# Work of GpSimd moved to VectorE, of VectorE to ScalarE, in three stages of a fused attention and expert kernel

## The chip, the cores and the metric

The kernel runs on one core of a Trainium2 chip, as one program. Its engines are TensorE (PE, matmuls and transposes), VectorE (DVE), ScalarE (ACT) and GpSimd (POOL); SyncE (SP) issues most of the DMAs. Each engine works through its own queue in order, and semaphores tie them together. The metric is the device time of one execution in microseconds (us).

## The reference

Three layers follow one another. Attention with 32 heads (4 batches x 8) over 1152 keys of 64 numbers, where pairs of queries are averaged first, leaves 576 x 4 = 2304 tokens of 512 numbers. A dense layer follows, and then a choice of one of eight experts for each token:

```
q_pool = q.reshape(B, H, S // 2, 2, D).mean(axis=3)
attn = softmax(q_pool @ k.T / 8);  x = attn @ v            # 2304 tokens x 512
h = x @ w_in;  g = h * sigmoid(1.702 * h);  x = g @ w_out   # 2048 hidden units
do = x @ w_skip > 0;  e = argmax(x @ w_gate)                # one of 8 experts
x[do] += p[e] * (relu(x[do] @ w1[e]) @ w2[e])               # 1024 hidden units
```

The result has to be right to float32. w_in and w_out come as 64-bit floats, all else as 32-bit floats.

## The kernel before, in words

All large products run in float32r, TensorE's rounded float format. To keep the precision, each operand is split into a high part (rounded, a ScalarE copy) and a low part (the rest, a subtraction), and a product is three matmuls: high x high, high x low, low x high.

**Attention** goes over 16 pairs of heads, 14 score units to a pair. Python code writes out the order: an agenda (`Agenda`) holds work for a later unit, and `quiet` puts work only on the units named in `AV_AT`. Beside it, the weights of the first of the 16 slices of the dense layer (`EARLY = 1`) are loaded and split in single steps (`weights`, L341).

**Splitting 64-bit weights** (`wsplit`, L422). A weight is two 32-bit words, 8 bytes from one to the next. Instructions on words build the high part: and with 0x7FFFFFFF (L450), shift (L451), max (L452), shift-or of the low word (L440) and its scaled copy on ScalarE (L441), shift-and (L454), or of the sign (L455), sign word (L444), and the low part's multiply (L445). The copy into the high part (L446, the put) follows one step later. The instructions stand in a list fq, and `fill(k)` takes the next k from it.

**The dense layer** (`ffn`, L484) goes over six chunks of tokens, 768, 384, 256, 256, 256 and 384, and in each over the 16 slices of 128 hidden units; a chunk of 768 has two pieces of 384 to a slice. One step is one piece of one slice: `layer1` has twelve matmuls into h, then Sigmoid (ScalarE, L568), g (VectorE, L569), its high half gh (ScalarE, L570) and its low half gl (L572). `layer2` follows two steps later with nine matmuls of 512 columns for a piece of 384. The weights stay in memory for all chunks and are split in the first one only, one half of a slice per step: that is the first pass, 32 steps of 21 matmuls. fill runs three of the list's instructions between g and gl, and four behind gl. Beside the end of a chunk the tokens of the next one are loaded (`xload`, SP queue), normalized (`xnorm`, L469) and split (`xhigh`, `xlow`).

**The experts** (`experts`, L841) take up to eight experts in turn, a slot each, and the tokens of a slot in tiles of 128. `tokens_tile` computes one: `up` (24 matmuls into two halves of h, hp), relu, transposes, the halves of hT (L928, L929), `down` (24 matmuls), and yo, which GpSimd's indirect DMA writes to the tokens' rows. In the first tile of a slot the weights of the next expert are split, 16 pieces (`splits`, L892): each is one ScalarE copy (L800) and one subtraction (L801). They stand in the queues between the parts of the tile: 3, 2, 2 and 2 pieces ahead of the second half's hT, 7 behind it. A weight buffer (stage) holds two pieces, and the load of the next expert but one fills it when both are split.

Of the kernel before, what the change touches and what calls it, by code (L numbers as in the profile page):

```python
# [71 lines left out]
class Kernel:  # L72
# [349 lines left out]
    def wsplit(self, fq, a, tmp, fb, k, ag=None):  # L422

        nc, V = self.nc, self.nc.vector
        hi_t, lo_t = self.W[fb, ("wih", "woh")[k]], self.W[fb, ("wil", "wol")[k]]
        if a.dtype == F32:
            def plain():
                nc.scalar.activation(hi_t, a, AF.Copy)  # L430
                V.tensor_tensor(lo_t, a, hi_t, op=ALU.subtract)
            fq.append(plain)
            return
        w = a.bitcast(U32).rearrange("p (n two) -> p n two", two=2)
        lo, hi = w[:, :, 0], w[:, :, 1]
        t1, t2, sg = tmp
        least = float(np.uint32(0x38000000).view(np.float32))

        def low():
            V.scalar_tensor_tensor(t1, lo, 9, t1, op0=ALU.logical_shift_right, op1=ALU.bitwise_or)  # L440
            nc.scalar.activation(t1.bitcast(F32), t1, AF.Copy, scale=2.0 ** -43)  # L441

        def last():
            V.tensor_scalar(sg, t2, 0xFF800000, None, op0=ALU.bitwise_and)  # L444
            (nc.gpsimd if fb else V).tensor_tensor(lo_t, t1.bitcast(F32), sg.bitcast(F32), op=ALU.mult)  # L445
            put = lambda: nc.scalar.activation(hi_t, t2.bitcast(F32), AF.Copy)  # L446
            put() if ag is None else ag.at(ag.now + 1, put)

        fq += [
            lambda: V.tensor_scalar(t2, hi, 0x7FFFFFFF, None, op0=ALU.bitwise_and),  # L450
            lambda: V.tensor_scalar(t1, hi, 23, None, op0=ALU.logical_shift_left),  # L451
            lambda: V.tensor_scalar(t2.bitcast(F32), t2.bitcast(F32), least, None, op0=ALU.max),  # L452
            low,
            lambda: V.tensor_scalar(t2, t2, 3, 0x3FFFF000, op0=ALU.logical_shift_left, op1=ALU.bitwise_and),  # L454
            lambda: V.scalar_tensor_tensor(t2, hi, 0xC0000000, t2, op0=ALU.bitwise_and, op1=ALU.bitwise_or),  # L455
            last,
        ]
# [11 lines left out]
        eng.tensor_tensor(x[:, :n], t[:, 0, :n], t[:, 1, :n], op=ALU.mult)  # L469

    def xtile(self, c, j, pc):
        i = (j * 2 + pc) if len(pieces(CH[c])) == 2 else (j * 2 + c % 2)
        n = pieces(CH[c])[pc][1]
        return [self.xhl[k][i][:, :n] for k in range(2)]

# [8 lines left out]
    def ffn(self, ctx):  # L484
# [59 lines left out]

        def xnorm(c, j, pc):
            xa[c, j, pc] = xr.tile([P, 384], F32, name="xa", tag="xa", bufs=4)
            self.xnorm(xa[c, j, pc], xraw.pop((c, j, pc)), c, j, pc, nc.gpsimd)

        def xsplit(c, j, pc):
            self.xhigh(xa[c, j, pc], c, j, pc)  # L550
# [4 lines left out]
        def layer1(c, fb, pc, fa, fb_):  # L555
            n = pieces(CH[c])[pc][1]
            h = hp.tile([P, 512], F32, name="h", tag="h")[:, :n]
            ah, al = self.W[fb, "wih"], self.W[fb, "wil"]
            k = 0
            for d in range(ND):  # L560
                xh, xl = self.xtile(c, d, pc)
                for a, x in ((ah, xh), (ah, xl), (al, xh)):
                    nc.tensor.matmul(h, a[:, d * P:d * P + P], x, start=(k == 0), stop=(k == 3 * ND - 1))  # L563
                    k += 1
            g = gp.tile([P, 384], F32, name="g", tag="g")[:, :n]
            gh = g3.tile([P, 384], F32R, name="gh", tag="gh")[:, :n]
            gl = g3.tile([P, 384], F32R, name="gl", tag="gl")[:, :n]
            nc.scalar.activation(g, h, AF.Sigmoid, scale=1.702)  # L568
            V.tensor_tensor(g, h, g, op=ALU.mult)  # L569
            nc.scalar.activation(gh, g, AF.Copy)  # L570
            fill(fa)
            (nc.gpsimd if c == 0 else V).tensor_tensor(gl, g, gh, op=ALU.subtract)  # L572
            fill(fb_)
            G[c, fb, pc] = (gh, gl)

# [147 lines left out]
        for g in range(len(steps) + LAG):  # L723
            ag.now = g
            if g < len(steps):
                c, fb, pc = steps[g]
                fa, fb_ = (2, 3) if CH[c] >= 384 else (1, 2)
                if g == 2:
                    self.recip(sm, B - 1, ag, 3)
                if c == 0:  # L730
                    if pc == 0:
                        fill(99)
                    wload(2 * (fb + EARLY) + 3 + pc)
                    wsplit(2 * (fb + EARLY) + 1 + pc)
                    fa, fb_ = 3, 4
                layer1(c, fb, pc, fa, fb_)
                if fb == 0 and pc == 0 and c + 1 < len(CH):
                    for j in range(ND):
                        for q in range(len(pieces(CH[c + 1]))):
                            g0 = first[0, 10] + 2 * j if c == 0 else first[c, 4] + 2 * j  # L740
                            ag.at(g0, xload, c + 1, j, q)
                            ag.at(g0 + 1, xnorm, c + 1, j, q)
                            ag.at(first[c, NF - 1] + 1 if c == 0 else g0 + 4, xsplit, c + 1, j, q)
            if g >= LAG:
                c2, f2, p2 = steps[g - LAG]
                layer2(c2, f2, p2)
                if f2 == NF - 1:
                    if c2 == 0 and p2 == 0:
                        rctx.close()
                        late["o"] = self.pool(ctx, "m_o", 2)  # L750
                        late["wg"] = late["o"].tile([P, 9, DM], F32, name="wg", tag="wg", bufs=1)
                        dma(late["wg"][:, 0:8], self.wgT.partition_broadcast(P))
                        dma(late["wg"][:, 8], self.w_skip.partition_broadcast(P))
                        for d in range(ND):
                            dma(wgd[:, d, 0:8], self.wgT[:, d * P:d * P + P].rearrange("e p -> p e"))
                            dma(wgd[:, d, 8:9], self.w_skip[d * P:d * P + P].rearrange("(p a) -> p a", a=1))
                    o, n = pieces(CH[c2])[p2]
                    grp = tuple((C0[c2] + o) // P + i for i in range(n // P))
                    if c2 < len(CH) - 1:
                        todo.extend((grp, i) for i in range(len(grp)))  # L760
            if g < len(steps) + LAG - 1:
                rstep()
                ag.run(g)
            if not (self.first or todo or fq or live[0]) and self.listed == NT - CH[-1] // P:

                self.first = late["o"].tile([P, 9, DM], F32, name="first", tag="wg", bufs=1)
                for m in range(4):
                    self.first_expert_load(m)
                for m in range(8):
                    ag.at(max(g + 2 + m // 2, first[len(CH) - 1, m] + LAG + 1), self.first_expert_split, m)  # L770

                ps = hp.tile([P, 8], F32, name="cn", tag="h")
                nc.tensor.matmul(ps, ONE, mac[self.listed], start=True, stop=True)
                V.tensor_scalar(self.early, ps[:, 0:1], P - 0.5, float(P), op0=ALU.is_gt, op1=ALU.mult)
                dma(self.ids_e, self.LIST[0:P])
                V.memset(self.x_e, 0.0)
                nc.gpsimd.indirect_dma_start(
                    out=self.x_e, out_offset=None, in_=self.X2[0:C0[-1]],
                    in_offset=bass.IndirectOffsetOnAxis(ap=self.ids_e[:, 0:1].bitcast(U32), axis=0),
                    bounds_check=C0[-1] - 1, oob_is_err=False,  # L780
                )
# [13 lines left out]
        fb, k = (s % 2) * 8 + q // 2, q % 2  # L795
        return self.W[fb, ("wih", "woh")[k]], self.W[fb, ("wil", "wol")[k]]

    def expert_split(self, s, q, raw, eng):
        hi, lo = self.piece(s, q)
        self.nc.scalar.activation(hi, raw, AF.Copy)  # L800
        eng.tensor_tensor(lo, raw, hi, op=ALU.subtract)  # L801

    def first_expert_load(self, m):
        t = self.first[:, m % 4 * 2:m % 4 * 2 + 2]
# [4 lines left out]

    def first_expert_split(self, m):  # L810
        for c in range(2):
            self.expert_split(0, 2 * m + c, self.first[:, m % 4 * 2 + c], self.nc.vector)
        if m < 4:
            self.first_expert_load(m + 4)

# [25 lines left out]
    def experts(self, ctx):  # L841
# [48 lines left out]
                dma(t, src)  # L890

        def splits(s):  # L892
            return [
                lambda q=q: self.expert_split(s, q, stage[q // 2][:, q % 2], nc.gpsimd if q % 3 == 2 else V)
                for q in range(16)
            ]

        def xpose(t):
            p = take("pt", pt)
# [8 lines left out]
        def tokens_tile(s, t, id2, x, ahead=(), more=(), behind=()):  # L908
# [35 lines left out]
            turned(0)  # L944
            some(A2)
            up(1, (2, 3))
            V.tensor_scalar(h[:, 512:], hp[1], 0.0, None, op0=ALU.max)
            for tn, xx in ahead:
                xput(xpose(tn), xx)
            some(A3)  # L950
# [100 lines left out]
```

## Time and profile before

| | us |
|---|---|
| three runs | 1127.57, 1119.11, 1115.97; median 1119.11 |
| the profiled execution | 1114.21, span 1112.4 |
| busy: TensorE | 1017.9 (91%) |
| busy: VectorE | 806.9 (73%) |
| busy: GpSimd | 581.1 (52%) |
| busy: ScalarE | 482.1 (43%) |

Attention goes to some 449 us, the first pass from there to 629, the other chunks to 902, the experts to the end. The shares of busy time are means over stages with different limits; what holds a stage is read in that stage. TensorE's granted clock was 0.966 of 2.4 GHz in the mean.

### The profile page before, as it was taken

Reading aid. Unit: us, or ns where it says so; the run is one execution under the profiler, and the core shown is the slowest. Engines: PE = TensorE matmul, PEld = TensorE weight load, DVE = VectorE, ACT = ScalarE, POOL = GpSimd, SP = SyncE. Lnnn points to the kernel's source line nnn. Section 1 sums busy time; section 2 is a strip of 40 time slices with the busy share of each in tenths; the row PEclk is TensorE's granted clock in tenths of the full one; section 3 lists DMA queues with packets and bytes.
Section 4 is the critical chain, followed back from the end, with each engine's and each line's share of the span. In section 5 each row is a group of like instructions: output and inputs, shape, how many; then the busy total and the mean of one; then the engine's idle time right before and its main releaser. Section 6 shows DMA issues by size and latency. Waiting matters only on the chain. (4 is left out here: it accounts for less than half of the span.)

```text
span 1112.4 us, 19158 instructions
## 1 busy us (share of the span) xinstructions
PE 1017.9 (91%) x7002; PEld 801.3 (72%) x7002; DVE 806.9 (73%) x1584; ACT 482.1 (43%) x885; POOL 581.1 (52%) x408
## 2 busy tenths in 40 slices
PE   6999999999999999688978999999999989977893
PEld 4766767666776666587867898888889877755672
DVE  6767787778877772699999589787567555578734
ACT  2555555555555545243333332333332334256432
POOL 3698888998999988444445202101110106156413
PEclk9999999999999999889999999999999989988897
DMA  4233332223333210332333420211211326456301
GB/s 154 66 95 80 92 108 77 76 90 91 92 108 93 71 48 27 125 96 95 105 117 100 143 77 20 69 62 31 66 41 55 111 92 215 149 184 214 112 31 39
DMA packets 64325, 103.39 MB, mean 93 GB/s; under 512 B 18630, under 2 KB 34630, under 8 KB 64072
## 3 DMA queue, kind: packets, MB, share of 16 engines
q1 hardware_dynamic: 60148, 96.35, 27.4%
q0 software_dynamic: 3904, 5.15, 1.5%
q8 instruction: 69, 1.13, 0.4%
q14 instruction: 56, 0.46, 0.1%
q10 hardware_dynamic: 148, 0.30, 0.1%
HBM read 90.04 MB, written 17.35 MB: 97 GB/s over the span
## 5 line engine op out<-in xcount | busy, mean ns | idle before, releaser
L230 DVE TENSOR_REDUCE mx<-xs 128x1 f32<-128x384 f32 x432 | 213.0, 549 | 79.5 <-PE xs L227 74.8
L271 ACT ACTIVATE E<-ss 128x640 f32<-128x640 f32 (+1 forms) x224 | 174.0, 786 | 155.3 <-PE ss L270 123.0
L286 POOL TENSOR_TENSOR acc<-acc,E 128x640 f32<-128x640 f32 (+1 forms) x96 | 182.1, 1897 | 19.5 <-ACT E L271 15.4
L563 PE MATMUL h<-xh,wih 128*128 128x384 f32 (+1 forms) x448 | 145.8, 326 | 30.8 <-ACT wih L446 26.0
L306 PE MATMUL av<-E,v 128*64 128x256 f32 (+1 forms) x1152 | 157.1, 413 | 0.0
L563 PE MATMUL h<-xl,wih 128*128 128x384 f32 (+1 forms) x448 | 143.6, 321 | 0.7 <-DVE xl L482 0.6
L563 PE MATMUL h<-xh,wil 128*128 128x384 f32 (+1 forms) x448 | 143.2, 320 | 0.0
L563 PEld LDWEIGHTS h<-xh,wih 128*128 128x128 f32 x448 | 86.7, 194 | 43.0 <-ACT wih L446 31.7
L306 PEld LDWEIGHTS av<-E,v 128*64 128x64 f32 x1152 | 75.7, 136 | 56.0 <-issue 15.1
L587 PE MATMUL acc<-woh,gh 128*128 128x512 f32 x288 | 115.6, 401 | 0.0
L589 PE MATMUL acc<-woh,gl 128*128 128x512 f32 x288 | 115.2, 400 | 0.0
L588 PE MATMUL acc<-wol,gh 128*128 128x512 f32 x288 | 114.9, 399 | 0.0
L227 PE MATMUL xs<-kh,qh 64*128 64x384 f32 x384 | 102.3, 389 | 9.7 <-ACT kh L207 7.2
L270 PE MATMUL ss<-qh,kh 64*128 64x320 f32 (+1 forms) x576 | 107.1, 340 | 0.9 <-ACT E L271 0.9
L270 PE MATMUL ss<-M,ONE 64*128 64x320 f32 (+1 forms) x576 | 95.0, 296 | 2.5 <-DMA M<-ml 2.3
L569 DVE TENSOR_TENSOR g<-h,g 128x384 f32<-128x384 f32 (+1 forms) x112 | 55.8, 498 | 56.0 <-ACT g L568 51.3
L606 DVE CUSTOM_DVE_ANT_0 junk<-xs,wg 128x512 bf16<-128x512 f32 x135 | 94.7, 701 | 2.0
L658 POOL DMA_INDIRECT LIST<-pay,si x18 | 18.3, 1018 | 143.0 <-DVE si L655 75.6
L270 PE MATMUL ss<-qh,kl 64*128 64x320 f32 (+1 forms) x576 | 92.4, 294 | 0.0
L270 PE MATMUL ss<-ql,kh 64*128 64x320 f32 (+1 forms) x576 | 92.4, 294 | 0.0
L568 ACT ACTIVATE g<-h 128x384 f32<-128x384 f32 (+1 forms) x112 | 49.1, 439 | 99.1 <-PE h L563 98.8
L563 PEld LDWEIGHTS h<-xl,wih 128*128 128x128 f32 x448 | 87.0, 194 | 5.2 <-DVE xl L482 1.2
(196 smaller groups left out, 2176.8 us busy)
## 6 DMA issues: line engine op xcount, KB each, us to landing
stage<-w SPq DMA_DIRECT2D x40, 512.0 KB
qd<-qT SPq DMA_DIRECT2D x16, 576.0 KB
v<-v SPq DMA_DIRECT2D x16, 576.0 KB
kr<-kT SPq DMA_DIRECT2D x15, 576.0 KB
wr<-w_in SPq DMA_DIRECT2D x15, 512.0 KB
wr<-w_out SPq DMA_DIRECT2D x15, 512.0 KB
X<-xs SPq DMA_DIRECT2D x18, 256.0 KB
out<-xs SPq DMA_DIRECT2D x18, 256.0 KB
```

The lines of the kernel that those rows point to most:

```text
L227: nc.tensor.matmul(ps[:, :384], q, k[:, part * 384:part * 384 + 384], start=True, stop=True)
L230: V.reduce_max(o, ps[:, :384], axis=AX.X)
L270: nc.tensor.matmul(ps[:, u, j * w:j * w + w], k[HALF[u]], q[HALF[u], qs], start=(n == 0), stop=(n == 3))
L271: nc.scalar.activation(place(p, i), ps[:, :, :len(kbs) * w], AF.Exp, scale=0.5 / D ** 0.5)
L286: G.tensor_tensor(d["a"], d["a"], place(p, i), op=ALU.add)
L306: nc.tensor.matmul(d["av"][HALF[u], :w], d["v"][:, u, kb], e[:, u, n * w:n * w + w], start=(kb == 0), stop=(kb == KB - 1))
L563: nc.tensor.matmul(h, a[:, d * P:d * P + P], x, start=(k == 0), stop=(k == 3 * ND - 1))
L569: V.tensor_tensor(g, h, g, op=ALU.mult)
L587: nc.tensor.matmul(acc[t], gh[:, ts], bh, start=(fb == 0), stop=False)
L588: nc.tensor.matmul(acc[t], gh[:, ts], bl, start=False, stop=False)
L589: nc.tensor.matmul(acc[t], gl[:, ts], bh, start=False, stop=(fb == NF - 1))
L606: V.tensor_tensor_reduce(out=junk, in0=R[grp[i]], in1=late["wg"][:, e], op0=ALU.mult, op1=ALU.add, scale=1.0, scalar=0.0, accum_out=R[grp] ...
```

## The change

In **wsplit** the and on VectorE gives way to an absolute value on ScalarE, issued when the list is made; the list has six entries instead of seven, in another order, and the low part's multiply is VectorE's everywhere. In the **dense layer's first pass** the subtraction for gl goes from GpSimd to VectorE, the next chunk's normalization too; the next chunk's tokens are loaded later, take the tiles of the first piece instead of the second, and are split one step earlier. In the **experts** all sixteen subtractions are VectorE's (five were GpSimd's), and the relu of the second half of h goes to ScalarE.

```diff
         def last():
             V.tensor_scalar(sg, t2, 0xFF800000, None, op0=ALU.bitwise_and)
-            (nc.gpsimd if fb else V).tensor_tensor(lo_t, t1.bitcast(F32), sg.bitcast(F32), op=ALU.mult)
+            (nc.gpsimd if 0 < fb < EARLY else V).tensor_tensor(lo_t, t1.bitcast(F32), sg.bitcast(F32), op=ALU.mult)
...
+        nc.scalar.activation(t2.bitcast(F32), hi.bitcast(F32), AF.Abs)
         fq += [
-            lambda: V.tensor_scalar(t2, hi, 0x7FFFFFFF, None, op0=ALU.bitwise_and),
             lambda: V.tensor_scalar(t1, hi, 23, None, op0=ALU.logical_shift_left),
+            low,
             lambda: V.tensor_scalar(t2.bitcast(F32), t2.bitcast(F32), least, None, op0=ALU.max),
-            low,
...
-        i = (j * 2 + pc) if len(pieces(CH[c])) == 2 else (j * 2 + c % 2)
+        i = (j * 2 + pc) if len(pieces(CH[c])) == 2 else (j * 2 + (c + 1) % 2)
...
-            self.xnorm(xa[c, j, pc], xraw.pop((c, j, pc)), c, j, pc, nc.gpsimd)
+            self.xnorm(xa[c, j, pc], xraw.pop((c, j, pc)), c, j, pc, V if c == 1 else nc.gpsimd)
...
-            (nc.gpsimd if c == 0 else V).tensor_tensor(gl, g, gh, op=ALU.subtract)
+            V.tensor_tensor(gl, g, gh, op=ALU.subtract)
...
-                            g0 = first[0, 10] + 2 * j if c == 0 else first[c, 4] + 2 * j
+                            g0 = first[0, 12] + 2 * j - 1 if c == 0 else first[c, 4] + 2 * j
                             ag.at(g0, xload, c + 1, j, q)
                             ag.at(g0 + 1, xnorm, c + 1, j, q)
-                            ag.at(first[c, NF - 1] + 1 if c == 0 else g0 + 4, xsplit, c + 1, j, q)
+                            ag.at(first[c, NF - 1] if c == 0 else g0 + 4, xsplit, c + 1, j, q)
...
-            return [
-                lambda q=q: self.expert_split(s, q, stage[q // 2][:, q % 2], nc.gpsimd if q % 3 == 2 else V)
-                for q in range(16)
-            ]
+            return [lambda q=q: self.expert_split(s, q, stage[q // 2][:, q % 2]) for q in range(16)]
...
-            V.tensor_scalar(h[:, 512:], hp[1], 0.0, None, op0=ALU.max)
+            nc.scalar.activation(h[:, 512:], hp[1], AF.Relu)
```

On VectorE one step of the first pass reads, before (from one g to the next; t are the word tiles, wr the loaded weights):

```order
L569 TENSOR_TENSOR g<-h,g 128x384
L450 TENSOR_SCALAR t_6303<-wr 128x512
L451 TENSOR_SCALAR t_6302<-wr 128x512
L452 TENSOR_SCALAR t_6303<-t_6303 128x512
L440 SCALAR_TENSOR_TENSOR t_6302<-wr,t_6302 128x512
L454 TENSOR_SCALAR t_6303<-t_6303 128x512
L455 SCALAR_TENSOR_TENSOR t_6303<-wr,t_6303 128x512
L444 TENSOR_SCALAR sg<-t_6303 128x512
L569 TENSOR_TENSOR g<-h,g 128x384
```

and with the change:

```order
L569 TENSOR_TENSOR g<-h,g 128x384
L451 TENSOR_SCALAR t_6302<-wr 128x512
L440 SCALAR_TENSOR_TENSOR t_6302<-wr,t_6302 128x512
L453 TENSOR_SCALAR t_6303<-t_6303 128x512
L572 TENSOR_TENSOR gl<-g,gh 128x384
L454 TENSOR_SCALAR t_6303<-t_6303 128x512
L455 SCALAR_TENSOR_TENSOR t_6303<-wr,t_6303 128x512
L444 TENSOR_SCALAR sg<-t_6303 128x512
L445 TENSOR_TENSOR wil_6083<-t_6302,sg 128x512
L569 TENSOR_TENSOR g<-h,g 128x384
```

The and (L450) is gone, gl stands behind the max (L453, before L452), and the low multiply (wil) closes the step; GpSimd has neither.

On ScalarE the same step, with the change (L449 is the absolute value, of the weights of the next entry of the list):

```order
L449 ACTIVATE t_6303<-wr 128x512
L568 ACTIVATE g<-h 128x384
L570 ACTIVATE gh<-g 128x384
L441 ACTIVATE t_6302<-t_6302 128x512
L446 ACTIVATE woh_6088<-t_6256 128x512
L449 ACTIVATE t_6350<-wr 128x512
```

Before, the four in the middle stood there alone, and the Sigmoid (L568) came right behind the put (L446) of the step ahead.

On VectorE the first tile of an expert slot, up to the second half of hT, before:

```order
L801 TENSOR_TENSOR wil_74<-stage_10712,wih_73 128x512
L801 TENSOR_TENSOR wol_76<-stage_10712,woh_75 128x512
L801 TENSOR_TENSOR wol_6093<-stage_10713,woh_6092 128x512
L801 TENSOR_TENSOR wil_6087<-stage_10714,wih_6086 128x512
L929 TENSOR_TENSOR hT<-pq_10734,hT 128x512
L801 TENSOR_TENSOR wil_6083<-stage_10715,wih_6082 128x512
L947 TENSOR_SCALAR h<-hp_10733 128x512
L906 TENSOR_TENSOR xT_10705<-pt_10730,xT_10705 128x512
L906 TENSOR_TENSOR xT_10707<-pt_10731,xT_10707 128x512
L801 TENSOR_TENSOR wol_6085<-stage_10715,woh_6084 128x512
L929 TENSOR_TENSOR hT<-pq_10735,hT 128x512
```

and with the change, from the third split on:

```order
L801 TENSOR_TENSOR wil_6091<-stage_10713,wih_6090 128x512
L801 TENSOR_TENSOR wol_6093<-stage_10713,woh_6092 128x512
L801 TENSOR_TENSOR wil_6087<-stage_10714,wih_6086 128x512
L926 TENSOR_TENSOR hT<-pq_10734,hT 128x512
L801 TENSOR_TENSOR wol_6089<-stage_10714,woh_6088 128x512
L801 TENSOR_TENSOR wil_6083<-stage_10715,wih_6082 128x512
L903 TENSOR_TENSOR xT_10705<-pt_10730,xT_10705 128x512
L903 TENSOR_TENSOR xT_10707<-pt_10731,xT_10707 128x512
L801 TENSOR_TENSOR wol_6085<-stage_10715,woh_6084 128x512
L801 TENSOR_TENSOR wil_6079<-stage_10716,wih_6078 128x512
L926 TENSOR_TENSOR hT<-pq_10735,hT 128x512
```

Three splits more stand ahead of the second hT (L929 before, L926 now), two more behind it, and the relu (L947) has left the queue.

## Rows read from the trace of the kernel before

**Rows 1.** Busy time by stretch, first pass: us, each engine's busy time, clock, DMA.
```profile
470.00:500.00 30.00, 24.36 (x107) 21.74 (x108) 29.07 (x48) 10.81 (x22) 13.71 (x12) 0.89 0.32 103
```

**Rows 2.** Order of time on ScalarE: start us, us, instruction; Sigmoids of steps 0, 29, 32 and later.
```profile
458.24 0.47 ACT L568 ACTIVATE g<-h 128x384 f32<-128x384 f32 x1
...
616.41 0.47 ACT L568 ACTIVATE g<-h 128x384 f32<-128x384 f32 x1
...
628.66 0.49 ACT L568 ACTIVATE g<-h 128x384 f32<-128x384 f32 x1 [2.17 <-PE h L563]
...
679.16 0.49 ACT L568 ACTIVATE g<-h 128x384 f32<-128x384 f32 x1 [2.54 <-PE h L563]
...
683.34 0.49 ACT L568 ACTIVATE g<-h 128x384 f32<-128x384 f32 x1 [2.24 <-PE h L563]
```

**Rows 3.** Order of time on VectorE at the first pass's start, GpSimd idle till 458.28.
```profile
454.91 0.43 DVE L450 TENSOR_SCALAR t<-wr 128x512 uint32<-128x512 uint32 x1 [11.84 <-DMA wr<-w_in]
455.25 0.42 DVE L451 TENSOR_SCALAR t<-wr 128x512 uint32<-128x512 uint32 x1
...
455.92 0.68 DVE L440 SCALAR_TENSOR_TENSOR t<-wr,t 128x512 uint32<-128x512 uint32 x1
456.52 0.42 DVE L454 TENSOR_SCALAR t<-t 128x512 uint32<-128x512 uint32 x1
456.97 0.69 DVE L455 SCALAR_TENSOR_TENSOR t<-wr,t 128x512 uint32<-128x512 uint32 x1
457.70 0.43 DVE L444 TENSOR_SCALAR sg<-t 128x512 uint32<-128x512 uint32 x1
458.74 0.56 DVE L569 TENSOR_TENSOR g<-h,g 128x384 f32<-128x384 f32 x1 [0.61 <-ACT g L568]
459.22 0.65 DVE L450 TENSOR_SCALAR t<-wr 128x512 uint32<-128x512 uint32 x1
```

**Rows 4.** Order of time on GpSimd and on VectorE, a later step of the first pass.
```profile
582.37 1.30 POOL L445 TENSOR_TENSOR wol<-t,sg 128x512 fp32r<-128x512 f32 x1 [2.55 <-ACT g L568]
583.62 1.20 POOL L572 TENSOR_TENSOR gl<-g,gh 128x384 fp32r<-128x384 f32 x1
...
582.83 1.13 DVE L450 TENSOR_SCALAR t<-wr 128x512 uint32<-128x512 uint32 x1
583.88 1.22 DVE L451 TENSOR_SCALAR t<-wr 128x512 uint32<-128x512 uint32 x1
```

**Rows 5.** VectorE: two splits, GpSimd idle; the low multiply in attention (busy, mean ns).
```profile
990.70 1.28 DVE L801 TENSOR_TENSOR wol<-stage,woh 128x512 fp32r<-128x512 f32 x2
...
L445 DVE TENSOR_TENSOR wol<-t 128x512 fp32r<-128x512 f32 x1 | 2.7, 2745 | 0.0
```

**Rows 6.** Waits of TensorE, 912 to 1112 us: total, times, longest.
```profile
PE y L937 <- DVE hT L929: 17.1, 4, 6.0
```

**Rows 7.** Order of time on VectorE and on GpSimd in one expert slot.
```profile
1023.80 6.19 DVE L801 TENSOR_TENSOR wol<-stage,woh 128x512 fp32r<-128x512 f32 x1
...
1023.24 1.30 POOL L801 TENSOR_TENSOR wil<-stage,wih 128x512 fp32r<-128x512 f32 x1
...
1028.19 1.25 POOL L801 TENSOR_TENSOR wil<-stage,wih 128x512 fp32r<-128x512 f32 x1
```

**Rows 8.** Order of time on TensorE: first matmuls of tiles; VectorE: the last yo.
```profile
958.55 0.39 PE L922 MATMUL hp<-wih,xT 128*128 128x512 f32 x1
...
972.10 0.50 PE L922 MATMUL hp<-wih,xT 128*128 128x512 f32 x1 [0.88 <-PEq L1007]
...
1052.85 0.39 PE L922 MATMUL hp<-wih,xT 128*128 128x512 f32 x1
...
1078.58 0.49 PE L922 MATMUL hp<-wih,xT 128*128 128x512 f32 x1 [0.56 <-PEq L1007]
...
1098.64 0.75 DVE L957 SCALAR_TENSOR_TENSOR yo<-y,ids,x_e 128x512 f32<-128x512 f32 x1 [1.17 <-PE y L937]
```

**Rows 9.** Busy time by stretch, weight loads in the experts: last columns clock, DMA share, GB/s.
```profile
1004.00:1020.00 16.00, 12.79 (x47) 10.10 (x48) 12.92 (x16) 7.81 (x15) 7.29 (x7) 0.79 0.80 264
```

More of the change, by code (lines that the diff above doesn't have):

```diff
@@ L796, in piece, with expert_split @@
         return self.W[fb, ("wih", "woh")[k]], self.W[fb, ("wil", "wol")[k]]
-    def expert_split(self, s, q, raw, eng):
+    def expert_split(self, s, q, raw):
         hi, lo = self.piece(s, q)
         self.nc.scalar.activation(hi, raw, AF.Copy)
-        eng.tensor_tensor(lo, raw, hi, op=ALU.subtract)
+        self.nc.vector.tensor_tensor(lo, raw, hi, op=ALU.subtract)
     def first_expert_load(self, m):
@@ L811, in first_expert_split @@
         for c in range(2):
-            self.expert_split(0, 2 * m + c, self.first[:, m % 4 * 2 + c], self.nc.vector)
+            self.expert_split(0, 2 * m + c, self.first[:, m % 4 * 2 + c])
         if m < 4:
```

## The prediction

> **What bounds the kernel now.** I read the page first, then the busy times by stretch, then the order of time on single engines. Attention (to 449 us) and the passes after the first one over the tokens (from 629 us) keep TensorE full, so nothing that the change does there can pay much. Two stages are left: the first pass over 768 tokens and the experts.
>
> In the first pass VectorE is the full engine: 29.07 of 30 us, TensorE 24.36, at a granted clock of 0.89 [rows 1]. A step there (one 384-token piece of one slice of 128 hidden units) is marked by ScalarE's Sigmoid. Step 0 has its Sigmoid at 458.24 us, step 29 at 616.41, step 32 (the first of the next pass) at 628.66; in the next pass the same matmuls take 683.34 - 679.16 = 4.18 us a step [rows 2]. So the first pass costs 170.4 us for 32 steps, where TensorE alone would need 134.
>
> Why VectorE is full shows when the same instructions are read with GpSimd idle and with GpSimd busy. With GpSimd idle, the and (L450) and the shift (L451) take 0.43 and 0.42 us [rows 3]; beside GpSimd's multiply of 1.30 us and its subtraction of 1.20 us they take 1.13 and 1.22 [rows 4]. The instructions are the same; some 1.5 us a step is time in which VectorE waits for GpSimd.
>
> In the experts, TensorE waited 17.1 us in four places for one VectorE instruction, the low half of hT (L929) [rows 6]. The order of time says why that one was late: the split ahead of it in VectorE's queue ran 6.19 us, from 1023.80 on, while GpSimd did five splits back to back from 1023.24 to 1029.44 [rows 7]. The same split takes 0.68 with GpSimd idle, and two of them 1.28 [rows 5].
>
> **The first pass, term by term.** Start to start with GpSimd idle [rows 3]: L450 to L451 0.34 (independent), L440 to L454 0.60, L454 to L455 0.45 and L455 to L444 0.73 (each needs the one before it), L569 to the next 0.48. The changed step on VectorE is g (0.48), shift (0.45, since the or that follows needs it; as L454), or (0.60), max (0.34), gl (0.48, the same shape as g), shift-and (0.45), or (0.73), sign (0.45), low multiply, and the next g. The low multiply of 128x512 is the one kind that VectorE never did undisturbed: 2.75 us beside GpSimd in attention above, and 0.60 below (two splits of that shape in 1.28, less the last one's end) [rows 5]. I take 0.60, since GpSimd now has nothing to do here; all of the other end would be 2.1 us a step. The sum is 4.58, say 4.6 us, against 5.34 now, so VectorE stays the bound, 0.4 above TensorE's 4.18.
>
> What is added on ScalarE hides: Abs, Sigmoid, gh, the scaled copy and the put are five instructions of 0.5 to 0.6 us in 4.6, and the Sigmoid starts at about 3.4 us after the g ahead of it (the or ends at 1.6, then the scaled copy, the put and Abs), 0.8 done before VectorE wants it. If that cover went, every tenth late would be a tenth a step.
>
> Step 28 is the last that splits weights: 28 x 4.6 = 128.8. The normalizing multiplies of the next pass's first tokens move from GpSimd to VectorE; two of the four fall before step 28, 0.55 each (as g): 1.1. The SP queue issues these token loads two to three steps later, one past the weight loads; each still has nearly two steps to land, so nothing. From step 28 to the Sigmoid of step 32 TensorE leads: the last w_in half is put 2.9 us into step 28 (the or ends at 1.6, then two copies of 0.6), then two steps of 4.18, then layer 1 alone, half a step's columns, 2.1, and 0.5 for the Sigmoid's lead over g at step 0 [rows 2, 3], together 13.9. The new place of the token tiles takes away the wait for them at step 32, which is inside this. Sum 143.8 against 170.4, less 0.5 for Abs ahead of the first Sigmoid: **-26 us**.
>
> **The experts.** Five splits of each round of sixteen go from GpSimd to VectorE (5 x 0.60 = +3.0), the relu of the second half goes to ScalarE (-0.6), and the stall goes (-5.5). An undisturbed tile without splits goes from 958.55 to 972.10, 13.55 us with the branch; four more transposes for the token tile ahead are 0.4: 14.0 a slot if TensorE sets it, 13.1 where no branch follows. Does TensorE set it? Ahead of the late hT VectorE loses 5.5 of stall and 0.6 of relu and gains three splits, 1.8, one of which falls into its present wait for the first relu: 4.9 earlier in all, where TensorE waited 5 to 6 in three of the four places [rows 6]. So next to nothing is left to wait for. From 972.10 to 1052.85 are four slots with splits, 80.75 us [rows 8]; they become 3 x 14.0 + 13.1 = 55.1: -25.6. In the last slot VectorE sets the end: yo starts 20.06 after the first matmul (1078.58 to 1098.64), 1.17 of it a wait for y [rows 8]; without that and the 5.5, with 2.4 more work of which 0.6 is hidden, it is 15.2, later than TensorE's 13.1: -4.9. The first slot loses the smallest of the four waits, 1. Together **-31.5**.
>
> **Attention.** VectorE loses two ands and ScalarE gains two Abs. The long multiply (2.75 us [rows 5]) moves one quiet step ahead. TensorE is full there, so I count 0, with the whole instruction either way as bounds: -2.7 to +2.7.
>
> **Rule and row.** Five GpSimd splits held one VectorE split for 6.19 us [rows 7]. The Trainium skill (SBUF — State Buffer, Who interferes with whom) says that a VectorE instruction with two SBUF inputs and a GpSimd instruction that reads SBUF take a shared port in turn, the second blocked until the first finishes. By that a split would be held for one GpSimd split, 1.3 us, not for five; the experts would give back some 7 us (five slots of 1.3) instead of 32 and the kernel would end near 1081. The row decides, and I keep 32.
>
> **The sum.** 1114.2 - 26 - 31.5 = 1056.7 us on the profiled execution's time. It was 4.9 below the median of the three runs and 1.8 below their fastest, so I add some 2.3: **1059 us**. The chance is 0.66.
>
> **Rivals.**
> - *Loads become the slots' bound* (0.11). One expert's weights are 4.2 MB; 16 us of them moved at 264 GB/s [rows 9], longer than the 14.0 slot. For: each stage buffer is refilled as it is freed. Against: now the refill stood still while a GpSimd split held a buffer, and there are 6 us of slack before the last piece is wanted. Three slots of 16 instead of 14: 1065.
> - *A new wait in the first pass* (0.13): gl on VectorE waits for gh, or Abs for its weights, 0.3 to 0.6 us a step. In the rows of before both are early by over half a microsecond. 28 x 0.45 = 13: 1072.
> - *VectorE does better than its sum* (0.06), and TensorE's 4.18 holds: 28 x 0.4 = 11 less: 1048.
> - *Slower: VectorE is saturated by its own work* (0.03). If the long rows are long from their own reads (weights 8 bytes apart, buffers just filled) and not from GpSimd, then nothing comes back: a step loses 1.05 for the and and gains 0.48 + 0.60, and each of five slots gains 3.0 - 0.6. It decides as soon as less than 0.1 us a step is freed: 28 x 0.03 + 2.2 + 5 x 2.4 = 15 more, 1132. The 0.42 with GpSimd idle [rows 3] speaks against it. The Trainium skill (Perfetto Trace Analysis, Optimizing Scalar/DVE Operations) takes that side: with VectorE saturated, handing work to ScalarE or even GpSimd may make sense; the same place adds that between VectorE and GpSimd, sharing a read port, it might not help, and rows 4 against rows 3 bear out the second half.
> - *It does only half of what it says* (0.01): the stalls go, but something else holds VectorE at the same place. About 1110.
>
> **Range.** The bounds of attention and the low multiply at 0.7 instead of 0.6 are +-3 each, the runs' own spread about 5. 1045 to 1078 takes in the first three rivals. A difference under 1% (11 us) is not told from none here: faster by over 1% 0.95, within 1% 0.02, slower 0.03.
>
> **What would show it.** Right: in the changed profile the Sigmoids of the first pass are 4.5 to 4.7 us apart; no VectorE split over 1 us in the experts; no wait of TensorE for hT over 1 us; slots of some 14 us; a granted clock near full in the first pass. Wrong: a wait of Abs for a weight load, with Sigmoids late behind it; the shift still over 1 us with GpSimd idle; ScalarE's splits waiting for the stage loads; gathers on the GpSimd queue landing late.

## The result, and the profile after

The changed kernel takes 1072.80 us (median of 4 runs, 1071.79 to 1075.09) against 1120.48 (4 runs, 1115.97 to 1127.57): a ratio of 0.957, 95% interval 0.952 to 0.963. The forecast was 1059, its range 1045 to 1078. The profiled execution took 1071.79 us, its span 1070.1; before, the span was 1112.4. So 42.3 us went, where the sum had 57.5.

| part, from the two profiles (us) | before | predicted | after |
|---|---|---|---|
| attention, to the last copy of the denominators (L323) | 450.7 | 450.7 | 454.0 |
| first pass, Sigmoid of step 0 to that of step 32 | 170.4 | 143.8 | 148.2 |
| slots 1 to 4 with splits, first matmul to first matmul of slot 4's second tile | 80.75 | 55.1 | 63.46 |
| last slot, first matmul to yo | 20.06 | 15.2 | 14.85 |
| first slot, first matmul to first matmul of slot 1 | 59.7 | 58.7 | 57.2 |

The stretches that are not in the table grew by 1.6 us together.

Lines behind the edited list of splits stand three lower than before: L926 is hT's low half, L919 the first product, L934 the second, L954 yo, L1004 the branch to a further tile.

**First pass.** The same stretch as in [rows 1]: its length, busy us of TensorE, of its weight loads, of VectorE, ScalarE and GpSimd, then granted clock, DMA share and GB/s.

```profile
470.00:500.00 30.00, 27.06 (x127) 23.88 (x127) 28.56 (x59) 17.53 (x32) 0.00 (x0) 0.94 0.33 106
```

GpSimd does nothing now. VectorE is still full, but with 59 instructions instead of 48. One step of it, in order of time on VectorE:

```profile
462.53 0.56 DVE L569 TENSOR_TENSOR g<-h,g 128x384 f32<-128x384 f32 x1 [0.37 <-ACT g L568]
463.01 0.42 DVE L451 TENSOR_SCALAR t<-wr 128x512 uint32<-128x512 uint32 x1
463.46 0.69 DVE L440 SCALAR_TENSOR_TENSOR t<-wr,t 128x512 uint32<-128x512 uint32 x1
464.07 0.42 DVE L453 TENSOR_SCALAR t<-t 128x512 f32<-128x512 f32 x1
464.40 0.55 DVE L572 TENSOR_TENSOR gl<-g,gh 128x384 fp32r<-128x384 f32 x1
464.87 0.42 DVE L454 TENSOR_SCALAR t<-t 128x512 uint32<-128x512 uint32 x1
```

The shift (L451), 1.22 us beside GpSimd in [rows 4], takes 0.42. In the grouped view over the pass, 28 of these shifts have a mean of 417 ns, and the low multiply, the kind for which there was no undisturbed row, 692 ns: start to start about 0.6, the lower bound that the sum took.

**Experts.** VectorE's splits and TensorE's waits from 880 us on, in the views by form (busy, mean ns) and of waits (total, times, longest):

```profile
L801 DVE TENSOR_TENSOR wol<-stage,woh 128x512 fp32r<-128x512 f32 x48 | 32.9, 686 | 13.2 <-ACT woh L800 10.1 <-issue 3.1
...
PE hp L919 <- PEq L1004: 7.6, 5, 2.4
...
PE y L934 <- ACT hT L925: 0.2, 1, 0.2
```

The 17.1 us for hT [rows 6] are gone and no split is long. What TensorE waits for now is its own sequencer ("PEq") at the branch between slots. In the order of time:

```profile
967.70 0.49 PE L919 MATMUL hp<-wih,xT 128*128 128x512 f32 x1 [1.98 <-PEq L1004]
...
980.67 0.40 PE L934 MATMUL y<-woh,hT 128*128 128x512 f32 x1
983.44 0.62 PE L919 MATMUL hp<-wih,xT 128*128 128x512 f32 x1 [2.37 <-PEq L1004]
983.86 0.63 PE L919 MATMUL hp<-wil,xT 128*128 128x512 f32 x1
```

Behind the wait of 2.37 the matmuls start 0.42 us apart instead of 0.23. Stretches of 4 us around it, with the columns of the first fence, show the clock:

```profile
980.00:984.00 4.00, 1.63 (x7) 1.01 (x6) 3.42 (x7) 2.01 (x5) 0.44 (x1) 0.96 0.89 289
984.00:988.00 4.00, 4.00 (x13) 3.14 (x12) 1.76 (x3) 0.71 (x2) 1.94 (x3) 0.62 1.02 344
988.00:992.00 4.00, 4.00 (x26) 3.37 (x25) 2.70 (x5) 3.67 (x8) 2.84 (x3) 1.00 0.67 224
```

13 matmuls fit where 26 fit 4 us later: most of 984 to 988 ran at 1.2 GHz. Slots 1 to 3 took 15.90, 15.74 and 16.92 us, not 14.0, and the first tile of slot 4 took 14.90, not 13.1.

### The profile page after: what moved, and what is told of

Same layout as the page of the kernel before. It is cut to its first block, busy times and chain, and to the rows that moved or that the text cites. A ratio compares the mean times of both kernels' runs of the same rounds, so it can differ in the third digit from the quotient of the medians.

```text
span 1070.1 us, 19067 instructions
## 1 busy us (share of the span) xinstructions
PE 1006.1 (94%) x7002; PEld 790.1 (74%) x7002; DVE 759.0 (71%) x1637; ACT 507.8 (47%) x928; POOL 461.9 (43%) x312
## 5 line engine op out<-in xcount | busy, mean ns | idle before, releaser
L563 PE MATMUL h<-xl,wih 128*128 128x384 f32 (+1 forms) x448 | 141.3, 315 | 0.2
L563 PE MATMUL h<-xh,wil 128*128 128x384 f32 (+1 forms) x448 | 140.9, 315 | 0.0
L469 POOL TENSOR_TENSOR xa<-xraw 128x256 f32<-128x256 f32 (+1 forms) x16 | 14.5, 906 | 264.8 <-DMA xraw<-RD 264.8
L563 PEld LDWEIGHTS h<-xh,wih 128*128 128x128 f32 x448 | 85.2, 190 | 30.7 <-ACT wih L446 16.9
L570 ACT ACTIVATE gh<-g 128x384 fp32r<-128x384 f32 (+1 forms) x112 | 53.7, 480 | 104.1 <-DVE g L569 104.1
L568 ACT ACTIVATE g<-h 128x384 f32<-128x384 f32 (+1 forms) x112 | 49.2, 439 | 95.9 <-PE h L563 95.8
```

## The experiments

Ratios are to the kernel before, timed on the same chip in the same session; its median moved between 1117 and 1127 from session to session, so kernels of one session are compared first.

### One part at a time

The first kernel is the one before with the experts' edits alone; the second is the changed one with the experts as before.

```diff
 # before, experts alone
-lambda q=q: self.expert_split(s, q, stage[q // 2][:, q % 2], nc.gpsimd if q % 3 == 2 else V)
+lambda q=q: self.expert_split(s, q, stage[q // 2][:, q % 2], V)
...
-V.tensor_scalar(h[:, 512:], hp[1], 0.0, None, op0=ALU.max)
+nc.scalar.activation(h[:, 512:], hp[1], AF.Relu)
```

> Kernel before with the expert layer's part alone: all sixteen splits of a slot on VectorE, the second relu on ScalarE. Theory (the parts add, each saves what its own stage shows): the expert layer falls from 202.3 to about 178 us, slots of 15.7 instead of 20.2, the time by 24.5, from 1120.5 to about 1096 (ratio 0.978). Rival (the weight loads or the branch set the slots, and the saving in the full change came from a different start of the stage): slots stay at 17 or more, the time falls by less than 14 (ratio over 0.987).

> The changed kernel with the expert layer's part as before: five splits of a slot on GpSimd, second relu on VectorE. Theory (the parts add): the first pass keeps its 148 us from Sigmoid 0 to 32, attention keeps its 3.3 us of loss, and the time is 1120.5 - 18 = about 1102 (ratio 0.984). Rival (the parts share a gain): under 10 us saved or over 26.

Experts alone: 1096.51 us, ratio 0.982 (0.979 to 0.986). First pass alone: 1095.94, ratio 0.982 (0.978 to 0.986). Against the session's median of 1117.03 they save 20.5 and 21.1 us, where 24.5 and 18 were expected. The product of the ratios, 0.964, is near the 0.957 of both, so the parts add within what the sessions differ. In the second profile TensorE's waits for hT are still there, "PE y L937 <- DVE hT L929: 27.3, 6, 6.0"; in the first they are gone. But the first had slots of 15.4 to 19.5 us (from yo to yo) with the changed kernel's expert code, and at the starts of three of them TensorE waited 3.1 to 3.5: the slots were not settled by VectorE alone.

### What holds TensorE between slots

My first theory was that the engines meet at the branch and TensorE waits there for VectorE's last split. If so, giving VectorE work for its idle time earlier in the slot shortens the slot.

```diff
-A0, A1, A2, A3 = 3, 2, 2, 2
+A0, A1, A2, A3 = 5, 0, 2, 2
```

> The changed kernel, with five splits instead of three ahead of a tile's first relu and none instead of two behind it. Theory A (a slot ends when VectorE has done its last split, since the engines meet at the branch between slots; VectorE loses 1.6 to 3.5 us per slot behind ScalarE's relu, which waits for TensorE): two splits (1.2 us) move into that wait, TensorE's wait at the boundary falls from 2.0-2.4 to about 1 us, its clock stays at 1.0 at the start of the slots, and slots go from 15.7 to about 14.4, some 5 us in all over slots 1 to 4 (ratio to the kernel before about 0.952). Rival B (the branch itself costs TensorE 2 us, whatever VectorE does): slots stay within 0.3 us, ratio 0.957. Rival C (the weight loads then bind): VectorE waits for the stage tiles, slots stay over 15.4.

1078.31 us, ratio 0.965 (0.960 to 0.971): not better. TensorE's waits at the slot starts were 2.94, 3.04 and 3.30 us, and the clock was down behind them (0.65, 0.50 and 0.50 over the next 3 us). VectorE's wait only moved: it waited 14.9 us in four places ahead of hT, where in the changed kernel it waits 10.1 us in four ahead of a split. So theory A fell. For weight loads it waited 1.4 us in one place, so rival C is out too, though the slots stayed over 15.4. Of rival B the kind fits, a price at the branch, but slots of 16.3 to 18.2 are not within 0.3 us: the price varies.

So I looked at the sequencer's own instructions at the branch line (PEldq in the rows). Each row gives count, shortest/median/longest ns, first and last start; the long one I take for the jump over the code of tiles that are not needed. After, and before:

```profile
L1004 PEldq COMPARE_BRANCH  x2: 176/1878/3580, 963.5 to 967.3; - x2
...
L1004 PEldq COMPARE_BRANCH  x2: 186/2072/3958, 978.9 to 983.1; - x2
```

```profile
L1007 PEldq COMPARE_BRANCH  x2: 176/2273/4370, 989.5 to 994.1; - x2
...
992.58 0.40 PE L937 MATMUL y<-woh,hT 128*128 128x512 f32 x1
994.44 0.49 PE L922 MATMUL hp<-wih,xT 128*128 128x512 f32 x1 [1.47 <-PEq L1007]
...
988.00:992.00 4.00, 2.97 (x7) 2.40 (x8) 3.98 (x7) 0.00 (x0) 0.00 (x0) 0.50 0.61 169
```

The jump was there before, and was no shorter: 4.37 us from 989.5, against 3.96 from 978.9 after. The difference is what covers it. It begins while matmuls already handed over still run. After, the last of them ends at 980.67 + 0.40 = 981.07, 2.2 us into the jump; before, at 992.98, 3.5 us into it, because the matmuls behind the wait for hT ran at a granted clock of 0.50. The first matmul follows the jump by 0.58 in both. So the wait is jump + 0.58 - cover: 3.96 + 0.58 - 2.18 = 2.36 after (2.37 in the row), 4.37 + 0.58 - 3.49 = 1.46 before (1.47 in the row). At the same slot end VectorE's own branch came at 981.6 and its semaphore at 983.3, behind TensorE's semaphore at 982.9, which took 0.05 us: VectorE waited there for TensorE, not the other way round. That the jump costs the time is theory D, and it can be tried: this input has at most one tile in slots 1 to 3, so the code behind that branch can be left out there. The edit takes out the branch with its code, so it prices the two together.

```diff
+                if s in (1, 2, 3):
+                    pass
-                if j + 1 < NJ:
+                elif j + 1 < NJ:
                     with tc.If(count[s] > P * (j + 1)):
```

> The changed kernel without the code for second and later token tiles in slots 1 to 3; this input never reaches it, so what is computed is the same, but at the end of these slots the engines no longer jump over that code. Theory D (new: TensorE's wait of 2.0 to 2.4 us at the start of a slot, and the half clock after it, come from its sequencer's jump at line 1004, which takes 3.6 to 4.0 us from 2.2 us before its last matmul ends, not from VectorE): the waits at the three slot starts fall below 0.7 us, no half clock at their start, slots go from 15.7-16.9 to about 14.0 to 14.4, together 5 to 7 us (time about 1066, ratio to before about 0.952). Theory A (TensorE waits for VectorE's last split at the slot's end): the waits stay at 2 us and the time stays within 1 us.

1061.68 us (1060.90 to 1063.58), 11 us less than the changed kernel's 1072.80 in another session. From slot 2 on a slot takes 13.1 us, read off yo (VectorE), and neither TensorE nor VectorE has room left (columns as above):

```profile
967.07 0.74 DVE L954 SCALAR_TENSOR_TENSOR yo<-y,ids,xg 128x512 f32<-128x512 f32 x1
980.21 0.73 DVE L954 SCALAR_TENSOR_TENSOR yo<-y,ids,x_e 128x512 f32<-128x512 f32 x1
993.32 0.74 DVE L954 SCALAR_TENSOR_TENSOR yo<-y,ids,xg 128x512 f32<-128x512 f32 x1
...
967.60:980.70 13.10, 13.10 (x66) 10.53 (x65) 12.96 (x22) 11.57 (x22) 6.44 (x5) 1.00 0.98 341
```

Slots 1 to 4 take 52.6 us (952.22 to 1004.81) where the sum had 55.1. That is 10.9 less than the 63.46 of the changed kernel: 6.4 are its three waits; about 3.2 are the half clock behind two of them, an estimate from 16 matmuls that start 0.43 apart instead of 0.23; 1.3 I can't assign. The weight loads at 341 GB/s hold nothing up in these slots: that rival is out. Is the jump's price really new? The same edit on the kernel before:

> The kernel before, without the code for second and later token tiles in slots 1 to 3 (never reached with this input). Theory D (the jump of 4.4 to 4.5 us was there before too, but hidden: TensorE's last matmuls ran at half clock behind its 6 us wait for VectorE, so more time of work was queued when the jump began): only the waits of 0.6 to 1.5 us at the slot starts go, slots 1 to 4 fall by 0.3 to 1.5 us each, 2 to 5 us in all against 11 in the changed kernel. Rival (the jump costs the same in both kernels): 8 us or more.

1118.57 us, ratio 0.995 (0.991 to 1.000); the interval runs from 0.3 to 10 us, so the time alone does not decide. Nor do the slots show a clear gain: slots 1 to 4 take 82.8 us from yo to yo instead of 84.2, but 82.0 instead of 80.75 from first matmul to first matmul; the run with the first pass alone, which has the same expert code as before, took 85.8 and 84.7. So the gain lies between -1.2 and 3.0 us: under the rival's 8, and at best at the low end of theory D's 2 to 5. The waits at the starts of slots 2 to 4 are gone, and TensorE waits for hT in all six slots, 30.3 us together, where it waited 17.1 in four: before, taking out the jump mostly moved its time into the wait for VectorE. The changed kernel unchanged, in the same session:

> The changed kernel unchanged, beside the others of this call. Its first slot ends had jumps of 3.6 to 4.0 us, other kernels with the same expert code 3.8 to 5.3. If the jump's time varies from one execution to the next, its profile shows slots 1 to 3 of 15.5 to 18.5 us and the time lies at 1070 to 1077.

1074.87 us (1073.11 to 1077.93), ratio 0.959 (0.953 to 0.965). Its jumps at the ends of slots 1 to 3 took 4.60, 3.76 and 4.64 us, the waits were 3.03, 2.20 and 3.12, and slots 1 to 4 took 65.7 us instead of 63.5. The jump does vary by about 1 us from one execution to the next.

### The relu, and GpSimd in small doses

> The changed kernel with the second relu of a tile back on VectorE (sixteen splits there as well). If the relu's place matters, VectorE's extra 0.6 us per tile comes ahead of the low part that TensorE needs: 0.3 to 0.6 us for each of 12 tiles, 3 to 7 us slower than the changed kernel. If TensorE's jump and clock set the slots and the last tiles have room, within 2 us of it.

```diff
-nc.scalar.activation(h[:, 512:], hp[1], AF.Relu)
+V.tensor_scalar(h[:, 512:], hp[1], 0.0, None, op0=ALU.max)
```

1077.90 us (1074.70 to 1079.89), 5 us above the changed kernel's first median and 3 above its repetition. TensorE waits 0.29 us for hT in each of five slots, 1.4 in all; its jumps took 4.6 to 5.3 us. The first reading has the right sign, but its size can't be told from the jumps'.

```diff
+lambda q=q: self.expert_split(s, q, stage[q // 2][:, q % 2], nc.gpsimd if q in (5, 10, 11) else V)
```

> The changed kernel with splits 5, 10 and 11 of a slot on GpSimd: one alone, and two in a row. If VectorE is held until the GpSimd instruction that came first is done and then has its turn, the longest VectorE subtraction beside either is about 0.7 + 1.3 = 2.0 us. If it is held through a whole run of GpSimd subtractions, it is 2.0 beside the single one and about 3.3 beside the pair (before: 6.2 through five). Time within 1% of the changed kernel, since VectorE is relieved of 1.8 us of a slot and held for as long.

One run, 1081.68 us; slots of 17.2 to 19.4 from yo to yo. In slots 1 to 5 the first reading is nearer. GpSimd and VectorE in the order of time, the pair and then a single one:

```profile
1002.25 1.29 POOL L801 TENSOR_TENSOR wil<-stage,wih 128x512 fp32r<-128x512 f32 x1 [3.35 <-ACT wih L800]
1003.50 1.73 POOL L801 TENSOR_TENSOR wol<-stage,woh 128x512 fp32r<-128x512 f32 x1
...
1016.52 1.32 POOL L801 TENSOR_TENSOR wol<-stage,woh 128x512 fp32r<-128x512 f32 x1
...
1002.38 1.71 DVE L801 TENSOR_TENSOR wol<-stage,woh 128x512 fp32r<-128x512 f32 x1
1004.01 1.77 DVE L801 TENSOR_TENSOR wil<-stage,wih 128x512 fp32r<-128x512 f32 x1
...
1015.99 2.41 DVE L801 TENSOR_TENSOR wil<-stage,wih 128x512 fp32r<-128x512 f32 x1 [0.34 <-ACT wih L800]
```

VectorE's first subtraction ends at 1004.09, inside the second GpSimd one, which is 0.44 us longer than the first: they take turns. Beside the single one it is 2.41, a little over 0.7 + 1.3. Even so, TensorE waits for hT again, 3.6 us in five places, the longest 1.25 in slot 4.

In slot 0 the same kernel does what the second reading says. A gather stood ahead of them in GpSimd's queue (0.99 us from 922.98), three subtractions followed it in a row, and one on VectorE was held through all of them:

```profile
923.98 1.32 POOL L801 TENSOR_TENSOR wol<-stage,woh 128x512 fp32r<-128x512 f32 x1
...
926.49 1.29 POOL L801 TENSOR_TENSOR wol<-stage,woh 128x512 fp32r<-128x512 f32 x1
...
923.38 4.96 DVE L801 TENSOR_TENSOR wol<-stage,woh 128x512 fp32r<-128x512 f32 x1
```

The number in a row is not what decides, for the kernel before shows both with two: held through both from 1044.37, and in turns at 1053.19, beside a GpSimd one of 1.74 us.

```profile
1044.37 2.99 DVE L801 TENSOR_TENSOR wil<-stage,wih 128x512 fp32r<-128x512 f32 x1 [0.35 <-ACT wih L800]
...
1053.19 1.77 DVE L801 TENSOR_TENSOR wol<-stage,woh 128x512 fp32r<-128x512 f32 x1
```

What decides between the two stays unexplained. In every held case here and in [rows 7] GpSimd's run began right behind a gather, but so did one run that took turns (961.87).

### The two smaller misses

The first pass ended 4.4 us later than forecast. ScalarE's Sigmoids of steps 29 to 33, then TensorE, VectorE and the SP queue around the gap, in the changed kernel:

```profile
596.98 0.47 ACT L568 ACTIVATE g<-h 128x384 f32<-128x384 f32 x1
600.93 0.47 ACT L568 ACTIVATE g<-h 128x384 f32<-128x384 f32 x1
608.60 0.47 ACT L568 ACTIVATE g<-h 128x384 f32<-128x384 f32 x1
610.22 0.47 ACT L568 ACTIVATE g<-h 128x384 f32<-128x384 f32 x1
614.24 0.49 ACT L568 ACTIVATE g<-h 128x384 f32<-128x384 f32 x1 [0.86 <-PE h L563]
...
608.75 0.44 PE L563 MATMUL h<-xh,wih 128*128 128x384 f32 x1 [1.42 <-ACT xh L478]
...
607.58 0.56 DVE L469 TENSOR_TENSOR xa<-xraw 128x384 f32<-128x384 f32 x1 [3.03 <-DMA xraw<-RD]
...
599.89 0.50 SPq L83 DMA_DIRECT2D xraw<-RD  x1
```

```diff
-g0 = first[0, 12] + 2 * j - 1 if c == 0 else first[c, 4] + 2 * j
+g0 = first[0, 11] + 2 * j - 1 if c == 0 else first[c, 4] + 2 * j
```

> The changed kernel with the second chunk's token loads and their multiplications two steps earlier, the split into high and low where it is. Theory (the step of 7.7 us between Sigmoids 30 and 31 is the fourth token load, issued one step ahead with 2 MB behind it): that step falls to about 4.2, TensorE's wait of 1.4 us in it goes, and the time falls by 1.4 to 3.5 us. Rival (the step is the eight high and low copies themselves): it stays over 6.5 and the time within 1 us.

```profile
597.08 0.47 ACT L568 ACTIVATE g<-h 128x384 f32<-128x384 f32 x1
601.04 0.47 ACT L568 ACTIVATE g<-h 128x384 f32<-128x384 f32 x1
604.22 0.47 ACT L568 ACTIVATE g<-h 128x384 f32<-128x384 f32 x1
608.04 0.49 ACT L568 ACTIVATE g<-h 128x384 f32<-128x384 f32 x1 [1.90 <-PE h L563]
612.23 0.49 ACT L568 ACTIVATE g<-h 128x384 f32<-128x384 f32 x1 [1.09 <-PE h L563]
```

The step of 7.67 us becomes 3.18 and TensorE's wait is gone; from step 0 (462.03 and 461.60) to step 33 it is 150.6 us instead of 152.2. From step 28 to step 32 it is 14.9 instead of 17.2, and up to step 28 0.5 more, since a third multiply falls before it. The mechanism is shown. The time, 1072.85 us (1068.77 to 1074.81), doesn't show it: this kernel's jumps took 4.6 to 5.5 us.

Attention ended 3.3 us later. In the changed kernel, VectorE and then TensorE:

```profile
135.29 1.55 DVE L444 TENSOR_SCALAR t<-t 128x512 uint32<-128x512 uint32 x1
136.88 1.67 DVE L445 TENSOR_TENSOR wil<-t 128x512 fp32r<-128x512 f32 x1
...
139.07 0.44 PE L227 MATMUL xs<-kh,qh 64*128 64x384 f32 x1 [1.45 <-DVE mx L230]
```

```diff
-        def last():
+        def sign():
             V.tensor_scalar(sg, t2, 0xFF800000, None, op0=ALU.bitwise_and)
+
+        def last():
...
+            sign,
             last,
```

> The changed kernel with the last two steps of a weight split (the sign mask and the low part's multiplication) apart in the list, seven entries as before instead of six. In the first pass the fills of 3 and 4 issue the same order. Theory A (attention's loss of 3.3 us comes from the two of them, 1.55 and 1.67 us in a row, falling into a step where VectorE has no room, with TensorE waiting 1.45 us for a maximum and a stretch at half clock after it): the last den copy of attention comes at about 451 instead of 454.0, and the time falls by about 3 us (ratio to before 0.954). Rival B (the loss comes from the first step on ScalarE or from the shift of every other step): it stays at 454 within 0.7.

Sign mask and multiply stood in one step before too, at 155.95, where TensorE waited 0.31 us, and again at 260.82, where it waited 1.83. The list of six steps instead of seven puts the pair one quiet step earlier, at 135.29 and 242.97, with waits of 1.45 and 1.41, and the clock falls to 0.66 behind the first (140 to 145 us). In either place the two in a row cost TensorE time. Apart, they start at 135.56 and 156.76, the wait is gone, and the last copy comes at 449.9 (theory A of this run, which had 451). The time is 1071.02 us, ratio 0.961 (0.956 to 0.965); with jumps of 3.8 to 4.5 us in it, the end of attention is the better witness. Over all profiles it came at 451.4 to 454.0 in eight executions of the changed order, at 450.7 to 452.0 in three of the old one, and at 448.8 to 449.9 in three with the steps apart. So the change cost attention 1.4 us in the mean; the other 2 of the 3.3 are spread between executions. The steps apart beat the old order too.

### The parts joined

```diff
-        for s in range(1, NE):
-            with tc.If(count[s] > 0):
-                slot(s)
+        def chain(s):
+            with tc.If(count[s] > 0):
+                slot(s)
+                if s + 1 < NE:
+                    chain(s + 1)
+        chain(1)
```

> The changed kernel with the two steps of a weight split apart, the second chunk's tokens two steps earlier, and the slots one inside the other, so that empty slots at the end are passed in one jump instead of two (slots are filled from the front, so a slot behind an empty one is empty). From the profile of the changed kernel: 1.6 to 2.1 us in the first pass, 0 to 3 in attention, 1.8 (one of GpSimd's rounds of semaphores) to 4.5 (TensorE's second jump) at the end: 1063 to 1069.

> The kernel of the run before it in this call, without the code for second and later tiles in slots 1 to 3, which this input never reaches: a bound for what the jumps cost in it, not a kernel for other inputs. Theory D: another 9 to 12 us, 1052 to 1058. If the jumps cost only their waits of 2 to 2.4 us as in the changed kernel's profile: 5 to 7 us.

1065.85 us (1064.84 to 1067.09), ratio 0.951 (0.945 to 0.956): 9 us under the changed kernel in the same session, and below both kernels. Its attention ended at 448.8 instead of 452.1, its first pass was 1.6 shorter up to step 33, and from the last yo to the end of the span it took 12.8 us instead of 14.0. That is 6.1 of the 9; another 3.1 lie between step 33 and the experts, in code that no part of this edit is meant to speed up, and this stretch varies from 279 to 283 us over the profiles. Without the unreached code, 1054.26 us (1050.85 to 1056.14), another 11.6: theory D's price once more, within one session, and slots 1 to 4 take 52.6 us again.

## Why the prediction was right, and where its sum was short

- *VectorE is slowed by GpSimd's company, not by its own work.* Right in both stages. All 28 steps run at the undisturbed durations of [rows 3]; most Sigmoids are 4.65 us apart (forecast 4.6), and no split of the experts is over 0.75 us. The rival that VectorE saturates itself is out, and so is that of a new wait in each step.
- *The low multiply at 0.60.* Right: mean 0.69 from start to end.
- *First pass: 143.8, measured 148.2.* Up to step 28 it is 131.0 against a forecast of 129.9, and from there to step 32 it is 17.2 against 13.9. Of these 3.3 the fourth token load is 2.3, since with the tokens earlier it is 14.9; the other 1.0 I can't assign. "Each still has nearly two steps to land, so nothing" was wrong for that one: its buffer is single, so it could go out only behind the third multiply, and 2 MB of gate weights were issued 1.2 us behind it.
- *Slots of 14.0, measured 15.9, 15.7 and 16.9.* This is the largest miss, with slot 4's first tile 8.4 of the 15 us. The term "13.55 us with the branch" was read from an undisturbed tile without splits that ends at slot 0's branch [rows 8], where the jump took 2.99 us and the weight loads were idle (6 GB/s between 968 and 972). At the ends of slots with loads it takes 3.6 to 5.5. The waits of 0.6 to 1.5 us that stood there before were short because matmuls that had come late behind the wait for VectorE, many of them at half clock, covered the jump: the stall that the change removed had been hiding another. Without the jump the mechanism gives 13.1 a slot, which is the sum's own figure for a slot with no branch behind it.
- *Last slot 15.2, measured 14.85.* Right.
- *Attention 0, bounds 2.7.* The mean loss is 1.4; the 3.3 of this profile lie outside the bounds. I followed the multiply to its new place but did not ask whether that step has room for it and the sign mask, which moves with it.
- *Loads as the slots' bound.* Out: 341 GB/s and slots of 13.1 without a wait. Whether they lengthen the jump is open (last section).
- *Rule and row.* I kept the row of five in a row (6.19 us [rows 7]) over turns of one instruction, 1059 over 1081; measured was 1072.8, short of 1059 for another reason. (The 1081 is on the profiled execution's time; on that of the 1059 it is 1084.) Keeping it was right: a stall from GpSimd's splits can't be left where GpSimd has no splits, and TensorE's wait for hT is gone. The kernel with three GpSimd splits shows turns of one in slots 1 to 5, VectorE instructions of 1.2 to 2.4 us beside GpSimd ones of 1.3 to 1.8, and a hold of 4.96 through three in slot 0. The Trainium skill (SBUF — State Buffer, Who interferes with whom) has the second instruction blocked until the first finishes; the turns agree with it, the holds through three (4.96) and five (6.19) don't.
- *The range, 1045 to 1078.* That it holds 1072.8 is in part luck. Its upper part was there for weight loads and for a new wait in the first pass (1072), and neither came; the jump that used it up was among no rival. Of the signs named, the Sigmoids, the splits and the waits for hT came as said; slots of some 14 us did not, and the clock in the first pass rose only from 0.89 to 0.94.

## What to carry to other kernels

Price an operation moved to an idle engine by what it does to the instructions beside it: here 16 splits on one engine beat 11 and 5 on two. When a long wait goes, look for what happened under it, branches and loads too, and subtract their cover from the gain. A jump costs TensorE its own time less the work already handed over, and that cover shrinks when the clock rises.

## What the runs showed of the hardware

- The branch over unreached code occupied TensorE's sequencer for 3.3 to 5.5 us, except where three tiles of a slot had run (0.45 to 0.93) and at the end of slot 0 (2.6 to 3.2). At full clock 2.2 us of matmuls ran on under it.
- Its length goes with one packet of 16 KB in a queue of the kind "instruction". Each of the 61 long jumps at this line in the 14 profiles has one that starts within it, and ends 1.2 to 1.6 us after it; the short ones behind three tiles have none. The packet starts 0.1 to 0.8 us into the jump at the end of slot 0, where the DMA engines are nearly idle (share 0.02 in the changed kernel), and 1.1 to 2.8 us into it at the ends of slots 1 to 3, beside the weight loads. For the jump at 978.9 in the changed kernel, the packet, and below it the DMA share (last column but one) at the end of slot 0 and here:

```profile
q8 instruction: 1, 0.02, 1.3%
...
948.40:951.20 2.80, 2.71 (x12) 1.86 (x10) 0.05 (x1) 0.00 (x0) 0.00 (x0) 1.00 0.02 6
978.90:982.90 4.00, 2.17 (x10) 1.41 (x8) 4.00 (x8) 2.15 (x5) 0.00 (x0) 1.00 0.86 285
```

No run changed the packet alone, so that the jump waits for it is not shown, and the jumps over the empty slots at the end take 3.9 to 5.3 us with the weight loads over.
- Waits of 2 to 3 us ahead of a slot's first matmul were followed by the clock at half in some slots (2.37 and 2.01, and 2.20 and 3.12 in the repetition) and not in others (1.98, and 3.03 in the repetition).
- One VectorE subtraction was held through five GpSimd ones in a row (6.2 and 7.2 us), through three (5.0) and through two (3.0), but in other places took turns with two (1.7 to 1.8 each). Why is open.
